# A convolution and feed-forward kernel: the turned filter block in a tile of its own ahead of the weights, taps and D in rows of 64, writes of H and K later

## The chip, the core and the metric

The kernel runs on one core of one Trainium2 chip. The core has five engines with instruction streams of their own: TensorE (PE) multiplies matrices into PSUM, VectorE (DVE) and ScalarE (ACT) do elementwise work and read PSUM, GpSimd (POOL) does small elementwise work and issues transfers, SyncE (SP) only issues transfers. A transfer (DMA) is put into the queue of the engine that issues it, and an engine that waits before an instruction holds everything behind that instruction. The metric is the device time of one execution in microseconds (us); lower is better.

## The reference

```python
def _A_ref(q, k, v, shift_k, ssm_k, ssm_D):       # S = 2048 tokens, D = 576 channels
    k_shift = sum of k moved down by 0..3 tokens, each times its tap shift_k[:, j]
    kv = k_shift * v
    y = causal convolution of kv with ssm_k over the tokens (by a Fourier transform of 2 S)
    return q * (y + kv * ssm_D)

def _B_ref(x, w_gate, w_up, w_down):              # 576 -> 4608 -> 576
    return (_gelu(x @ w_gate) * (x @ w_up)) @ w_down

x = A_q
x = x + _A_ref(_layernorm(x), A_k, A_v, A_shift_k, A_ssm_k, A_ssm_D)
x = x + _B_ref(_layernorm(x), B_w_gate, B_w_up, B_w_down)
x = x + _A_ref(_layernorm(x), A_k, A_v, A_shift_k, A_ssm_k, A_ssm_D)
x = x + _B_ref(_layernorm(x), B_w_gate, B_w_up, B_w_down)
```

(Four lines of it are told in words.) All inputs and the output are bf16. The convolution does not depend on x, so it is computed once and used in both layers.

## The kernel before

The tokens are worked in four blocks of 512 (`BS`), each as four tiles of 128 (`RT`). The convolution is done by blocks: a block of kv and a block of the filter are each taken into a frequency form by matmuls with tables of cosines and sines (`W`, `Wx`), multiplied on VectorE, and brought back by matmuls. The frequency forms are called K (of kv) and H (of the filter); they are kept in DRAM (`Kd`, `Hd`) because later blocks need them again. `kc` and `h0` are the tiles that hold K and H of block 0 until they are written. Block m of the output needs K of the blocks 0 to m and H of the blocks m to 0, and with them two neighbouring products are added.

The feed-forward part goes in units of 512 tokens and one layer, and in three parts (`NP`) of the 4608 hidden columns: twelve tiles of hidden columns are made by matmuls with the gate and up weights (`gu`, L1673 for the first unit's first part, L1755 otherwise), then multiplied by the down weights (`dn`, L1789). The weights are loaded in groups of four tiles, `load_wgu(n)` (three transfers on SP's queue, L1193 to L1195; three buffers) and `load_wd(n)` (L1203).

The program is written by hand in the order in which each engine shall run it. `begin` (L831) is the startup: it makes kv of block 0, H and K of block 0 and the first 512 tokens' gated input, with each matmul and copy in a written order. Then `first_half` (L1601) makes the first half of the first hidden tiles: six steps of 36 matmuls (`half_gu`), for the two tiles of 128 tokens that are ready first; while they run the other two tiles are normalized (`norm0`), turned on TensorE (`turn0`) and copied (`copy0`). The loop of L1739 makes the second half. From there on a planner with estimated costs (`Pace`, `fill`) decides between which matmuls a piece of the convolution of blocks 1 to 3 is put; its decisions are made when the program is built, not while it runs.

The names that the change touches:

- The filter lies in DRAM as channels by tokens. For blocks 1 to 3 it is turned by transposing loads. For block 1 this is done in `begin` (L975 to L981): `hx`, a scratch tile that takes a buffer of `xnT` (the same buffers hold `kT` and `dg` before), takes four transposing loads of 128 tokens in its first half; the result is written to DRAM (`Td[1]`), and read back into its second half in the order of tokens that the matmuls need. `hT1` is that second half. All of these transfers are on SP's queue. `hT1` is first used by the pieces `rest` (L829), the first of which the planner puts behind the first step of the second half; their matmuls are those of L282.
- `head.more(k)` (L1582) issues loads on SP's queue: x of block 0 for k = 0, weight groups 0 and 1 for k = 1, group 2 for k = 2. The down weights are loaded behind `begin` (L1598).
- The taps `shift_k` and the vector D come to one row of `sk1` and `dvec`; twelve matmuls with a one spread the taps of the first 384 channels over the partitions (L889 to L893, copied to `wcol`), two spread those of the last 192 over all partitions (L906, copied to `sx`), five spread D (L914, copied to `dcol`). For the later blocks `taps_out` (L984) reorders the taps on GpSimd by four copies on one row, writes them to DRAM (`skT`), and a transfer spreads them over all partitions (`skc`, L1083). `load_k(1)` and `load_v(1)` load k and v of block 1.
- `put(kt, ...)` (L1021) writes `h0[kt]` or `kc[kt]` to DRAM by a transfer on GpSimd's queue; eight such writes stand in `begin`. `h0[0]` lies in a buffer that the pieces `rest` borrow for their sums, `h0[1]` to `h0[3]` in those of `kr`, into which K is loaded again (L547); `kc` lies in the buffers that K of block 1 takes (L254).

Of the kernel before, what the change touches and what calls it, by code (L numbers as in the profile page):

```python
# [18 lines left out]
BF16 = mybir.dt.bfloat16  # L19
# [3 lines left out]
P = 128  # L23
# [63 lines left out]
class Conv:  # L87
# [743 lines left out]
    def begin(self, head, tables):  # L831
# [4 lines left out]
        with ExitStack() as es:  # L836
            tmp = es.enter_context(tc.tile_pool(name="s_tmp", bufs=1))
            AT = 96
            sk1 = tmp.tile([AT + 1, D, KS], BF16, name="sk1")
            dvec = tmp.tile([1, D], BF16, name="dvec")  # L840
# [5 lines left out]
            ones = tmp.tile([AT + 1, P], BF16, name="ones")  # L846
# [11 lines left out]

            nc.vector.memset(full, 1.0)
            nc.vector.memset(ones[:], 1.0)  # L860
            nc.vector.memset(sk1[0:AT, nt * P:, :], 0.0)
            nc.scalar.dma_start(out=sk1[AT:AT + 1, :, :].rearrange("p d j -> p (d j)"), in_=self.sk.rearrange("d j -> (d j)").unsqueeze(0))
            self.load_k(0, nc.sync)
            nc.scalar.dma_start(out=dvec[:], in_=self.sD.unsqueeze(0))
# [10 lines left out]
            nc.sync.dma_start(out=self.W[:, 12:24, :], in_=tables[:, 12:24, :])  # L875
            head.more(1)

# [11 lines left out]
            for db in range(nt):  # L889
                for j in range(KS):  # L890
                    nc.tensor.matmul(ps[:, 0, db * KS + j:db * KS + j + 1], lhsT=sk1[AT:AT + 1, db * P:(db + 1) * P, j],
                                     rhs=ones[AT:AT + 1, 0:1],
                                     start=True, stop=True)  # L893
            nc.vector.tensor_copy(out=wcol[:].rearrange("p b j -> p (b j)"), in_=ps[:, 0, 0:nt * KS])
# [9 lines left out]
            cuts = ((0, P), (P, DW))  # L904
            for e, (lo, hi) in enumerate(cuts):
                nc.tensor.matmul(ps[:, e, 0:(hi - lo) * KS], lhsT=ones[:], rhs=sk1[:, nt * P + lo:nt * P + hi, :].rearrange("p d j -> p (d j)"),  # L906
                                 start=True, stop=True)
            for e, (lo, hi) in enumerate(cuts):
                nc.scalar.copy(out=sx[:, :, lo:hi], in_=ps[:, e, 0:(hi - lo) * KS].rearrange("p (d j) -> p j d", j=KS))
# [3 lines left out]
            at = DW  # L913
            for db in range(nd + 1):  # L914
                nc.tensor.matmul(px[0:width(db), 1, at + db:at + db + 1], lhsT=dvec[:, db * P:db * P + width(db)], rhs=ones[0:1, 0:1],
                                 start=True, stop=True)
# [12 lines left out]
            nc.scalar.copy(out=kx[:, 2, :], in_=px[:, 1, 0:DW])  # L929
            for dbs, pt in zip(DBS, pts):  # L930
                ne = len(dbs)
                if dbs is DBS[1]:
                    nc.scalar.copy(out=dcol[:, 0:nd], in_=px[:, 1, at:at + nd])
                    nc.scalar.copy(out=dcol[0:D - nd * P, nd:nd + 1], in_=px[0:D - nd * P, 1, at + nd:at + nd + 1])
# [40 lines left out]
            hx = head.scratch([P, 2, RT, D], "hx")  # L975
            for i in range(RT):
                nc.sync.dma_start_transpose(out=hx[:, 0, i:i + 1, :], in_=self.hk[:, BS + i * P:BS + (i + 1) * P])  # L977
            head.more(2)
# [904 lines left out]
```

## Time and profile before

| | us |
|---|---|
| median of 3 runs | 916.75 |
| lowest, highest | 911.25, 917.38 |
| profiled execution, its time | 916.24 |
| profiled execution, span of the core | 914.3 |
| startup up to the first matmul of the feed-forward part | 33.65 |
| wait of TensorE in front of L282 | 4.94 |

The profile is one execution taken by the hardware profiler. Its page gives the busy time of each engine, the queues' transfers and the chain of waits that ended last; further views give the instructions in order of time (the timeline: start, length, engine, line, operation, what it writes and reads, and in brackets the idle time before it and what ended it), who waited for whom, the transfers with their time from issue to landing, and the busy time of each engine in chosen stretches (windows). PE is TensorE's matmuls, PEld its loading of weights; a queue's name ends in q. A line number is that of the kernel before.

### The profile page before, as it was taken

What the parts mean: (1) busy time and instruction counts of PE and PEld (TensorE: products, weight loads), DVE (VectorE), ACT (ScalarE), POOL (GpSimd) and SP (SyncE); (2) the same over time, 40 slices, a digit from 0 to 9 for tenths busy, and PEclk for the clock granted to TensorE, in tenths of its full rate; (3) what the DMA queues carried; (4) which work ended last, traced back from release to release, by engine and by line L of the source; (5) the groups of instructions that cost most, each with busy time, mean ns of one, the idle gap of its engine ahead of it and who ended that gap; (6) DMA issues with size and microseconds to landing.
All of it is one profiled execution on the core that took longest, in us unless ns stands there. A gap on an engine that the chain in (4) does not pass through costs nothing.

```text
span 914.3 us, 19185 instructions
## 1 busy us (share of the span) xinstructions
PE 902.3 (99%) x8143; PEld 525.5 (57%) x8143; DVE 576.8 (63%) x985; ACT 328.9 (36%) x618; POOL 160.2 (18%) x339
## 2 busy tenths in 40 slices
PE   9979999999999999999999999999999999999998
PEld 7766556465565564664655655646646546556555
DVE  8978987679788885697898855443333335333332
ACT  7745534633324255353124133551121224321211
POOL 4502504220114031330114002220000003100000
PEclk9999999999999999999999999999999999999999
DMA  9999995938428508784915700870620721967620
GB/s 250 329 265 236 281 264 116 230 130 195 157 80 226 144 14 150 228 156 99 278 54 127 189 10 32 179 153 20 137 79 2 155 79 27 180 161 175 140 59 27
DMA packets 132025, 132.90 MB, mean 145 GB/s; under 512 B 46114, under 2 KB 123619, under 8 KB 131940
## 3 DMA queue, kind: packets, MB, share of 16 engines
q1 hardware_dynamic: 121728, 94.65, 46.2%
q0 software_dynamic: 10208, 37.02, 12.7%
q8 instruction: 63, 1.03, 0.5%
q14 instruction: 22, 0.18, 0.1%
q10 hardware_dynamic: 4, 0.01, 0.0%
HBM read 108.35 MB, written 12.39 MB: 132 GB/s over the span
## 4 chain that ended last, share of the span: by engine, by line
PE 94%; DMA 4%; DVE 1%; SPq 1%; ACT 0%; issue 0%; ACTq 0%
PE gu L1755 59%; PE dn L1789 31%; DMA Td<-hx 2%; PE gu L1673 1%; DMA hx<-Td 1%; PE cps L282 1%; SPq L977 1%; PE ps L282 1%; DMA hx<-in_A_ssm_k_dram 0%; PE ps L415 0%; PE cps L415 0%; PE cps L885 0%; DVE v L991 0%; DVE wx L948 0%; DVE wx L947 0%; ACT h L1010 0%
## 5 line engine op out<-in xcount | busy, mean ns | idle before, releaser
L1755 PE MATMUL gu<-xnT,wgu 64*128 64x512 bf16 x4968 | 540.7, 377 | 0.0
L1755 PEld LDWEIGHTS <-wgu 64*128 64x128 bf16 x4968 | 240.1, 94 | 293.9 <-issue 6.2
L1764 ACT ACTIVATE ga<-gu 128x512 f32<-128x512 f32 x258 | 153.9, 596 | 451.1 <-PE gu L1755 442.7
L1765 DVE TENSOR_TENSOR hT<-ga,gu 128x512 bf16<-128x512 f32 x258 | 177.1, 687 | 200.4 <-ACT ga L1764 198.9
L1789 PE MATMUL dn<-wd,hT 128*128 128x288 bf16 x2304 | 292.2, 287 | 0.0
L1789 PEld LDWEIGHTS <-hT 128*128 128x128 bf16 x2304 | 223.4, 98 | 65.7 <-issue 9.5
L1828 DVE TENSOR_TENSOR x_c<-x_c,dn 128x576 f32<-128x576 f32 x62 | 46.7, 753 | 55.2 <-PE dn L1789 54.9
L1231 POOL TENSOR_SCALAR nm<-s 128x1 f32<-128x1 f32 x56 | 20.1, 358 | 267.4 <-DVE x_c L1820 210.8
L1239 ACT ACTIVATE junk<-x_c,nm 128x576 bf16<-128x576 f32 x48 | 36.9, 769 | 28.4 <-POOL nm L1231 25.9
L1247 POOL TENSOR_TENSOR rstd<-ve,neghalf_t 128x1 f32<-128x1 f32 x58 | 37.5, 647 | 4.8
L555 POOL DMA_DIRECT2D hr<-Hd x32 | 17.4, 545 | 118.0 <-DVE prod L361 118.0
L1303 ACT ACTIVATE xn<-x_c,nb,rstd 128x576 bf16<-128x576 f32 (+1 forms) x48 | 28.6, 644 | 5.9 <-POOL nb L1251 5.7
L285 ACT COPY eo<-cps 128x576 f32<-128x576 f32 x29 | 18.6, 642 | 31.6 <-PE cps L282 28.3
L1246 POOL TENSOR_SCALAR ve<-ss 128x1 f32<-128x1 f32 x58 | 21.3, 367 | 47.2 <-ACT junk L1239 47.1
L1811 DVE TENSOR_TENSOR ob<-x_c,dn 128x576 bf16<-128x576 f32 x15 | 11.3, 754 | 29.0 <-PE dn L1789 29.0
L1652 ACT ACTIVATE ga<-gu 128x512 bf16<-128x512 f32 x26 | 15.5, 597 | 34.5 <-PE gu L1755 25.9
L1673 PE MATMUL gu<-xnT,wgu 64*128 64x256 bf16 x432 | 26.3, 279 | 0.6 <-ACT xnT L1485 0.6
L1673 PEld LDWEIGHTS <-wgu 64*128 64x128 bf16 x432 | 22.0, 98 | 4.4 <-issue 1.4
L362 DVE TENSOR_TENSOR prod<-prod 128x576 bf16<-128x576 bf16 x48 | 22.0, 458 | 1.7
L430 POOL DMA_DIRECT2D out_dram<-ob x12 | 6.8, 563 | 91.8 <-issue 47.0
L245 DVE SCALAR_TENSOR_TENSOR eo<-eo 128x576 f32<-128x576 f32 x22 | 16.3, 753 | 5.8 <-ACT eo L285 5.8
L1281 DVE SCALAR_TENSOR_TENSOR x_c<-g_t,rstd,x_c 128x576 f32<-128x576 f32 x16 | 13.0, 815 | 8.6 <-POOL rstd L1247 8.6
(188 smaller groups left out, 589.9 us busy)
## 6 DMA issues: line engine op xcount, KB each, us to landing
wgu<-in_B_w_gate_dram SPq DMA_DIRECT2D x45, 576.0 KB, 5.6
wd<-in_B_w_down_dram SPq DMA_DIRECT2D x30, 864.0 KB, 6.8
wgu<-in_B_w_up_dram SPq DMA_DIRECT2D x45, 512.0 KB, 7.9
hr<-Hd POOLq DMA_DIRECT2D x32, 288.0 KB, 4.8
kr<-Kd POOLq DMA_DIRECT2D x24, 288.0 KB, 5.0
Kd<-kc POOLq DMA_DIRECT2D x12, 288.0 KB, 6.3
k<-in_A_k_dram POOLq DMA_DIRECT2D x3, 1008.0 KB, 13.5
wgu<-in_B_w_up_dram SPq DMA_DIRECT2D x45, 64.0 KB, 7.4
```

The source lines that it names most:

```text
L362: nc.vector.tensor_tensor(out=dst, in0=pr[:, 0, :], in1=pr[:, 1, :], op=ALU.subtract if part == 0 else ALU.add)
L1231: nc.gpsimd.tensor_scalar(out=v["nm"][:], in0=v["s"][:], scalar1=-1.0 / D, scalar2=None, op0=ALU.mult)
L1239: nc.scalar.activation(out=junk[:], in_=get_x(), func=ACT.Square, bias=v["nm"][:, 0:1], accum_out=v["ss"][:])
L1246: nc.gpsimd.tensor_scalar(out=ve[:], in0=v["ss"][:], scalar1=1.0 / D, scalar2=EPS, op0=ALU.mult, op1=ALU.add)
L1247: nc.gpsimd.tensor_tensor(out=v["rstd"][:], in0=ve[:], in1=neghalf_t[:, 0:1], op=ALU.pow)
L1303: nc.scalar.activation(out=xn[:, lo:hi], in_=x_c[c][:, j, 0:hi - lo], func=ACT.Identity, scale=v["rstd"][:, 0:1], bias=v["nb"][:, 0:1])
L1673: nc.tensor.matmul(pair[:, s, e * 256:(e + 1) * 256], lhsT=w[r0:r0 + HK, k, gi * P:(gi + 1) * P], rhs=xnT[r0:r0 + HK, blk_of[k], tok], sta ...
L1755: nc.tensor.matmul(pair[:, s, :], lhsT=w[r0:r0 + HK, k, gi * P:(gi + 1) * P], rhs=xnT[r0:r0 + HK, b, :], start=(k == 0), stop=(k == NKC - 1))
L1764: nc.scalar.activation(out=ga[:], in_=pair[:, 0, :], func=ACT.Gelu_apprx_tanh)
L1765: nc.vector.tensor_tensor(out=hT[:, fi, :], in0=ga[:], in1=pair[:, 1, :], op=ALU.mult)
L1789: nc.tensor.matmul(part[h][:, h, 0:HW], lhsT=hT[:, fi, at * P:(at + 1) * P], rhs=wd[2 * wb + fi // WT][:, fi % WT, h * HW:(h + 1) * HW], s ...
L1828: nc.vector.tensor_tensor(out=xh, in0=xh, in1=acc[:, :, 0:HW], op=ALU.add)
```

## The change

The turned filter block gets a tile `hx` of its own, in the startup's pool, so its four transposing loads no longer wait for a buffer. They are issued on SP's queue behind the last table and in front of weight group 0; the write to `Td[1]` follows group 0, and groups 1 and 2 follow the write. The readback stays where it was, in a scratch tile without the first half.

The taps and D are loaded as nine rows of 64 channels, each row twice side by side. Four matmuls with columns of the identity spread the taps of 384 channels (two copies, one for each half of the partitions), three those of the last 192, and D comes by one transpose, with its copies ahead of those of `kT`. `taps_out` is one copy on nine rows, and `load_k(1)` follows it at once. The spread of the taps, `skc`, is issued behind the scales of the first two tiles.

The eight writes of H and K leave `begin`: one is issued in step 1 of `first_half` in the place of `load_x(1)`, four in step 2 behind the accumulating transfers, three in step 2 of the second half, with `load_x(1)` behind them. The two tiles that are turned in steps 2 and 3 of `first_half` are turned in steps 3 and 4.

```diff
-            AT = 96
-            sk1 = tmp.tile([AT + 1, D, KS], BF16, name="sk1")
-            dvec = tmp.tile([1, D], BF16, name="dvec")
+            HP = P // 2
+            NH = D // HP
+            sk9 = tmp.tile([NH, 2, HP * KS], BF16, name="sk9")
+            dv9 = tmp.tile([NH, 2, HP], BF16, name="dv9")
+            sk9t = tmp.tile([NH, KS, HP], BF16, name="sk9t")
+            hx = tmp.tile([P, RT, D], BF16, name="hx")
...
+            nc.scalar.dma_start(out=sk9[:], in_=twice(self.sk.rearrange("(b p) j -> b (p j)", p=HP)))
             self.load_k(0, nc.sync)
-            nc.scalar.dma_start(out=dvec[:], in_=self.sD.unsqueeze(0))
+            nc.scalar.dma_start(out=dv9[:], in_=twice(self.sD.rearrange("(b p) -> b p", p=HP)))
...
             nc.sync.dma_start(out=self.W[:, 12:24, :], in_=tables[:, 12:24, :])
+            for i in range(RT):
+                nc.sync.dma_start_transpose(out=hx[:, i:i + 1, :], in_=self.hk[:, BS + i * P:BS + (i + 1) * P])
             head.more(1)
+            nc.sync.dma_start(out=self.Td[1].rearrange("(t p) d -> p t d", p=P), in_=hx[:])
+            head.more(2)
...
+            for j in range(KS):
+                nc.tensor.matmul(ps[:, 0, 2 * nt * j:2 * nt * (j + 1)], lhsT=sk9[:].rearrange("b h (p j) -> b (h p) j", j=KS)[:, :, j], rhs=self.ident[0:NH, 0:2 * nt], start=True, stop=True)
+            for h, (lo, hi) in enumerate(halves):
+                nc.vector.tensor_copy(out=wcol[lo:hi], in_=ps[lo:hi, 0, 0:2 * nt * KS].rearrange("p (j b h) -> p b j h", b=nt, h=2)[:, :, :, h])
...
+            for c in range(DW // HP):
+                nc.tensor.matmul(ps[:, c // 2, c % 2 * HP * KS:(c % 2 + 1) * HP * KS],
+                                 lhsT=self.ident[0:NH, 2 * nt + c:2 * nt + c + 1].to_broadcast([NH, P]),
+                                 rhs=sk9[:, 0, :], start=True, stop=True)
...
+            nc.tensor.transpose(pt[:, 1, 0:NH], dv9[:].rearrange("b h p -> b (h p)"), self.ident[0:NH, 0:NH])
...
-            hx = head.scratch([P, 2, RT, D], "hx")
-            for i in range(RT):
-                nc.sync.dma_start_transpose(out=hx[:, 0, i:i + 1, :], in_=self.hk[:, BS + i * P:BS + (i + 1) * P])
-            head.more(2)
-            nc.sync.dma_start(out=self.Td[1].rearrange("(t p) d -> p t d", p=P), in_=hx[:, 0])
-            self.hT1 = hx[:, 1]
+            self.hT1 = head.scratch([P, RT, D], "hT1")[:]
             nc.sync.dma_start(out=self.hT1, in_=self.Td[1].rearrange("(p i) d -> p i d", i=RT))
...
-                for j in range(KS):
-                    nc.gpsimd.tensor_copy(out=self.skc[AT:AT + 1, j, :], in_=sk1[AT:AT + 1, :, j])
-                nc.gpsimd.dma_start(out=skT[:], in_=self.skc[AT:AT + 1, :, :].rearrange("p j d -> p (j d)"))
+                nc.gpsimd.tensor_copy(out=sk9t[:], in_=sk9[:, 0, :].rearrange("b (p j) -> b j p", j=KS))
+                nc.gpsimd.dma_start(out=skT[:].rearrange("o (j b p) -> (o b) j p", j=KS, p=HP), in_=sk9t[:])
+                self.load_k(1, nc.gpsimd)
...
             kacc(0)
-            put(0, h0, kc)
-            put(2, h0)
+            nc.gpsimd.dma_start(out=self.skc[:].rearrange("p j d -> p (j d)"), in_=skT[:].broadcast_to([P, KS * D]))
...
+            def put_at(n):
+                for kt, what in (((0, (h0,)),), ((0, (kc,)), (2, (h0, kc)), (1, (h0,))), ((1, (kc,)), (3, (h0, kc))))[n]:
+                    put(kt, *what)
+            self.put_at = put_at
...
-                for n in range(2):
+                load_wgu(0)
+            else:
+                for n in range(1, 3):
                     load_wgu(n)
-            else:
-                load_wgu(2)
...
                     sq0(3)
-                    load_x(1)
+                    conv.put_at(0)
                     root0(3)
-                elif n in (2, 3):
+                elif n in (2, 3, 4):
...
                         conv.together0(conv.A0)
+                        conv.put_at(1)
...
-                    conv.run_p()
-                    j = 2 * n - 3
-                    turn0(j)
-                    copy0(j, nc.scalar.copy)
-                    t.on_act(1.4, t.pe)
+                    if n < 4:
+                        conv.run_p()
+                    if n > 2:
+                        j = 2 * n - 5
+                        turn0(j)
+                        copy0(j, nc.scalar.copy)
+                        t.on_act(1.4, t.pe)
...
                     if n == 0:
                         conv.window = t.pe + 0.6
+                    elif n == 2:
+                        conv.put_at(2)
+                        load_x(1)
```

More of the change, by code (lines that the diff above doesn't have):

```diff
@@ L888, in begin @@
             ps = new()
-            for db in range(nt):
-                for j in range(KS):
[L891 to L894, printed above, removed]
+            halves = ((0, HP), (HP, P))
+            for j in range(KS):
+                nc.tensor.matmul(ps[:, 0, 2 * nt * j:2 * nt * (j + 1)], lhsT=sk9[:].rearrange("b h (p j) -> b (h p) j", j=KS)[:, :, j], rhs=self.ident[0:NH, 0:2 * nt], start=True, stop=True)
+            for h, (lo, hi) in enumerate(halves):
+                nc.vector.tensor_copy(out=wcol[lo:hi], in_=ps[lo:hi, 0, 0:2 * nt * KS].rearrange("p (j b h) -> p b j h", b=nt, h=2)[:, :, :, h])
             def diagonals(db, js=range(KS)):
@@ L903, in begin @@
             ps = new()
[L904 to L908, printed above, removed]
+            for c in range(DW // HP):
+                nc.tensor.matmul(ps[:, c // 2, c % 2 * HP * KS:(c % 2 + 1) * HP * KS],
+                                 lhsT=self.ident[0:NH, 2 * nt + c:2 * nt + c + 1].to_broadcast([NH, P]),
+                                 rhs=sk9[:, 0, :], start=True, stop=True)
+            for e, (lo, hi) in enumerate(((0, P), (P, DW))):
                 nc.scalar.copy(out=sx[:, :, lo:hi], in_=ps[:, e, 0:(hi - lo) * KS].rearrange("p (d j) -> p j d", j=KS))
@@ L912, in begin @@
             px = new()
[L913 to L916, printed above, removed]
             for i in range(KS - 1):
@@ L1075, in begin @@
             kacc(2)
-            put(2, kc)
             kfwd(1, 0, small())
@@ L1082, in begin @@
             kfwd(1, 1, new())
-            nc.gpsimd.dma_start(out=self.skc[:].rearrange("p j d -> p (j d)"), in_=skT[:].broadcast_to([P, KS * D]))
-            self.load_k(1, nc.gpsimd)
             apart(1, 0)
```

15 lines of the change are left out of this document (4 added, 11 removed).

## The prediction

> **What bounds the kernel now.** I read the page first, then who TensorE waits for over the whole span, then the chain of waits around the longest of those waits, then each queue's timeline in the first 90 us. Page, then waits of PE:
>
> ```profile
> span 914.3 us, 19185 instructions
> PE 902.3 (99%) x8143; PEld 525.5 (57%) x8143; DVE 576.8 (63%) x985; ACT 328.9 (36%) x618; POOL 160.2 (18%) x339
> ...
> PE cps L282 <- DMA hx<-Td: 4.9, 1, 4.9
> PE cps L885 <- DVE wx L859: 1.2, 1, 1.2
> PE xps L1478 <- DVE hT L1679: 0.9, 1, 0.9
> PE ps L415 <- DVE yb L362: 0.8, 1, 0.8
> PE gu L1673 <- ACT xnT L1485: 0.6, 1, 0.6
> PE cps L219 <- DVE v L991: 0.3, 1, 0.3
> ```
>
> TensorE is idle for 914.3 − 902.3 = 12.0 us, and the six waits (4.9 + 1.2 + 0.9 + 0.8 + 0.6 + 0.3 = 8.7) are all in the first 56 us; most of the rest is the tail behind the last matmul. So behind the startup only TensorE's own work counts, and this change, which keeps that work, is worth what it does to those waits. The large one, from the chain (start, us, what):
>
> ```profile
> 22.66 4.41 DMA hx<-in_A_ssm_k_dram
> ...
> 27.21 19.40 DMA Td<-hx
> ...
> 46.62 8.34 DMA hx<-Td
> ...
> 55.80 3.54 PE gu L1673 x36
> ...
> 59.69 2.07 PE gu L1673 x36
> ```
>
> The filter block is turned by four transposing loads, written to DRAM (19.40 us for 576 KB), read back (8.34 us) and landed at 46.62 + 8.34 = 54.96. TensorE's next step needed it. Behind the wait the same 36 matmuls took 3.54 instead of 2.07 us. TensorE's timeline gives the wait, and a window the clock (the third number from the end, PEclk):
>
> ```profile
> 55.01 0.40 PE L282 MATMUL cps<-hx,W 128*128 128x288 bf16 x2 [4.94 <-DMA hx<-Td]
> ```
> ```profile
> 55.00:60.00 5.00, 5.00 (x50) 3.21 (x51) 0.00 (x0) 1.79 (x4) 0.00 (x0) 0.66 0.94 338
> ```
>
> TensorE stood from 55.01 − 4.94 = 50.07 on. 5.00 × (1 − 0.66) = 1.70 us of full-speed work is lost to the clock granted after it. The stall costs 4.94 + 1.70 = 6.64 us in all.
>
> **Turned block (L975 to 981).** SP's queue, and three rows of the DMA answer for 27.2 to 46.6:
>
> ```profile
> 4.78 0.65 SPq L1193 DMA_DIRECT2D wgu<-in_B_w_gate_dram  x1
> ...
> 9.07 0.60 SPq L1193 DMA_DIRECT2D wgu<-in_B_w_gate_dram  x1
> ...
> 10.85 3.01 SPq L1195 DMA_DIRECT2D wgu<-in_B_w_up_dram  x1
> 14.04 10.31 SPq L977 DMA_TRANSPOSE hx<-in_A_ssm_k_dram  x4
> ...
> 27.21 1.48 SPq L979 DMA_DIRECT2D Td<-hx  x1
> ```
> ```profile
> q0 software_dynamic: 1286, 4.72, 72.6%
> q1 hardware_dynamic: 1717, 1.76, 30.9%
> ...
> Td<-hx SPq DMA_DIRECT2D x1, 576.0 KB, 19.4
> ```
>
> The write took 19.40 us while POOL's queue (q0) moved 4.72 MB against 1.76 MB of SP's (q1). Before, hx took the buffer of kT and dg and stood in the text behind the work on them. With a tile of its own it follows the last table load, in the place of group 0 of the weights, at 4.78. From first issue to last landing they took 22.66 + 4.41 − 14.04 = 13.03: landed at 17.8. SP issues them until 4.78 + 10.31 = 15.1, then group 0 of the weights (4.78 to 9.07: 4.3 us) until 19.4, so the write of Td goes out at 19.4. Priced as before it lands at 19.4 + 19.40 = 38.8 and the readback at 38.8 + 8.34 = 47.1, still 3 us ahead of 50.07. It should be less, since the eight H and K writes that POOL queued in that stretch are gone from it. I take the wait as gone: **−4.94 and −1.70**. What remains as bound: nothing gone (0) if the write were 3 us longer than 19.40 and everything else as bad.
>
> What the transposes and the write are moved past: groups 0, 1 and 2. Their landing rows of before (groups 1 and 2, last piece), and TensorE's needs:
>
> ```profile
> wgu<-in_B_w_up_dram SPq DMA_DIRECT2D x1, 64.0 KB, 12.5
> wgu<-in_B_w_up_dram SPq DMA_DIRECT2D x1, 64.0 KB, 14.6
> ...
> 33.65 6.15 PE L1673 MATMUL gu<-xnT,wgu 64*128 64x256 bf16 x108 [0.56 <-ACT xnT L1485]
> 40.71 0.66 PE L1478 MATMUL xps<-ident,xn 128*128 128x128 bf16 x9 [0.92 <-DVE hT L1679]
> ```
>
> Two steps of 2.07 use one group. Group 0 is needed at 33.65 and issued by 19.4: 14 us for it. Group 1 is needed at 33.65 + 2 × 2.07 = 37.8; issued behind the write (1.48) from 20.9 on, with its last piece 10.85 − 9.07 = 1.8 later at 22.7, it lands at 22.7 + 12.5 = 35.2. Group 2 goes out 14.04 − 9.07 = 5.0 behind it, last piece at 27.7, lands at 27.7 + 14.6 = 42.3, and is needed at 33.65 + 4 × 2.07 + 0.92 + 0.66 = 43.5. So 1.2 us are to spare at prices of which the 14.6 was paid beside the H and K writes; **0**, bound +2. The down weights, which stood behind SP's wait for Td, come earlier: 0.
>
> A rule bears on this: the Trainium skill, "DMA: Bandwidth & Descriptors", Latency and other measured facts, gives a transposing load 261 GB/s. By it, the block's 576 KB are an estimated 2.3 us, and the weights would slip by that, not 10.3. The trace disagrees (10.31 us of issuing), so the row stands; by the page's figure the weights rival below would all but vanish.
>
> **POOL's queue.** Tap rows, moved steps, the next writer of kc's slots, and landings of H in the crowded stretch and of K over the whole span:
>
> ```profile
> 13.87 2.65 POOL L986 COPY skc<-sk 1x576 bf16<-1x576 bf16 x4
> ...
> 39.12 0.74 POOL L1208 DMA_DIRECT2D x_b<-in_A_q_dram  x1
> ...
> 43.68 2.63 POOL L389 DMA_DIRECT2D yb<-yb  x3 [2.05 <-DVE yb L382]
> 45.30 2.15 POOL L547 DMA_DIRECT2D kr<-Kd  x2
> ...
> 74.16 1.56 DVE L254 TENSOR_TENSOR kc<-eo 128x288 bf16<-128x288 f32 x4
> ```
> ```profile
> Hd<-h POOLq DMA_DIRECT2D x2, 288.0 KB, 14.4
> ...
> Kd<-kc POOLq DMA_DIRECT2D x12, 288.0 KB, 6.3
> ```
>
> Four copies of 0.7 us on one row become one on nine rows (a fifth as many elements per row: bounded by 0.2 and 0.7 us); POOL stands off the chain there, so 0. k of block 1 goes out behind the taps at about 16, the shared taps behind the scales near 23; both are earlier than VectorE needs them, 0. The H and K writes: H of row 0 now goes at 39.12 in the place of x_b. Behind it ACT's first lent tile (slot of h0[0]) is wanted at 50.07 + 0.4; at 14.4 us it would land at 53.5, 3 us late, at an undisturbed few us well ahead. ACT then holds up; TensorE can run on into two further psum pairs (2 × 2.07) before it feels it. 0, bound +1. Four writes follow the accumulating transfers, where the kr loads went (45.30): out at 45.30 + 4 × 0.88 = 48.8 (2.63 / 3 for one issue). Then the first kr load waits on POOL for the K write and for h0[1]'s slot; behind it stand the second kr load, three writes (kc 1, h0[3], kc 3) and x_b of block 1. Landed in 6.3: 55.1, two kr issues (2.15) and three writes (2.6) to 59.9, landed at 66.2; kc's slots are next written at 74.16 − 6.64 = 67.5. So 0, with 1.3 us to spare; at 14.4 for both landings 82.4, 15 late: rival 2. H and K issues also leave 23 to 30, where VectorE's chain runs; 0.
>
> **Startup rows.** Rows of the first matmuls and of what follows:
>
> ```profile
> 3.06 0.56 PE L891 MATMUL ps<-ones,sk 1*128 1x1 bf16 x12
> 4.30 0.40 PE L915 MATMUL ps<-ones,dvec 1*128 1x1 bf16 x5
> ...
> 3.66 0.17 DVE L894 COPY wcol<-ps 128x12 f32<-128x12 f32 x1 [1.79 <-PE ps L891]
> ```
>
> Twelve tap matmuls become four: 8 × (0.49 / 12) = −0.3. One wcol copy becomes two: +0.1 to +0.17. The three matmuls for the taps of the last columns move 768 columns as the two did: 0. The five for D go, one transpose comes, behind the k transposes; the D copies on ACT stand before the kT copies, +0.3 there, hidden by TensorE's h transposes. If nine rows, twice, land later than the one row did: D's row, issued behind the taps, was first used at 4.30, so the taps are there by then against 3.06: +1.2. Ends −0.3 and +1.2; I take **0**, nearest to the matmul rows, which did not wait.
>
> **Turns one step later (L1633).** Step 3's matmuls now take the slot that waited 0.92; that wait stays. Step 3 ends at 40.71 + 2.07 = 42.8, the first turn (0.6) at 43.4, step 4 at 45.45; the second turn then wants the psum slot of step 3, which VectorE frees here:
>
> ```profile
> ...
> 45.13 0.68 DVE L1679 TENSOR_TENSOR hT<-ga,gu 128x512 bf16<-128x512 f32 x1
> ```
>
> 45.13 + 0.68 = 45.81: **+0.36** (0 if VectorE is earlier).
>
> **Sum.** 916.24 (the profiled execution: 914.3 span and 1.94 around it, 0.51 below the median 916.75) − 4.94 − 1.70 + 0.36 = 909.96, so 910.0. What is late next: nothing by 6.64; VectorE, which worked on through the stall, idled 5.72 behind it until TensorE's next products came:
>
> ```profile
> 60.49 0.69 DVE L1656 TENSOR_TENSOR hT<-ga,hT 128x1024 bf16<-128x1024 bf16 x1 [5.72 <-ACT hT L1653]
> ```
>
> That is all but 0.9 of the 6.64, and what it does in the step behind (61 to 68) TensorE wants only one step later.
>
> **Rivals.**
> 1. *Weights late (slower).* SP issues group 1 behind the landing of the transposes, and the transposes stand behind all of the first loads:
>
> ```profile
> W<-twiddles SPq DMA_DIRECT2D x1, 384.0 KB, 8.5
> ```
>
> That last table, issued just ahead of 4.78, landed 8.5 later, at about 12.8. If the transposes move only then and take their 13.03 from there, they land at 25.8, Td goes out at 25.8, group 1 from 27.3 (last piece 29.1), and with 14.6 it lands at 43.7: 5.9 late, and 1.70 of clock: 909.96 + 7.6 = 917.6 (with 12.5, 915.5; with Td's 19.40, 922.4). For: issues of 3.01 us for a piece of 64 KB show that SP's queue backs up. Against: those 13.03 held two groups of weights that were in front, and POOL's eight writes have left the stretch behind. It costs from a landing of group 1 at 37.8 on and turns the sign at 42.4. The Trainium skill, "DMA: Bandwidth & Descriptors", Queues, rings and completion order, says that each DMA engine takes the queues' packets in turn; the row's 72.6 to 30.9 is a worse share for SP than an even turn, so with k, the taps and v in POOL's queue the trace speaks for this rival more than the page does.
> 2. *A new wait behind POOL's queue.* At the lent tile, H of row 0 lands at 53.5: ACT 3 us late, TensorE 1 to 3: 911 to 913. At kc's slots, VectorE is late by what the two landings take beyond 12.6 + 1.3; TensorE goes on for the three psum pairs of down products, 9.3 us (24 matmuls each; the 36 of 2.07 are 18 pairs of half height side by side, so 0.115 for 256 columns and 0.129 for 288); at 14.4 twice 15 − 9.3 and the clock's 1.70, 7.4: 917.4. For: the writes now stand beside the down weights. Against: POOL's queue got the larger share.
> 3. *The wait stays in part.* Td goes out at 25.8 as in rival 1, takes 19.40 and 8.34, and is back at 53.5, or sooner: 1 to 3.4 us late, with some of the clock: 911 to 915. That the change does nothing to the wait: 916.
> 4. *More goes.* VectorE frees the psum slots earlier and the taps' −0.3 come through: −0.36 − 0.92 − 0.3: 908.4, and 907 if the write-free stretch from 23 to 30 gives another us.
>
> **Chances.** Forecast 0.60; rival 1 0.10; rival 2 0.11; rival 3 0.07; rival 4 0.12. The measurement can tell about 1% (9.2 us, 907.6 and 925.9). Faster by over 1%: rival 4 by half, the forecast by a fifth (it needs 2.4 us more): 0.06 + 0.12 = 0.18. Slower by over 1%: rival 1 beyond its 922.4, half of it, 0.05. Within: 0.77. The range goes from 906.5 (rival 4's end with half a us of measurement) to 916 (rival 3 and the first half of 2): rival 1, the second half of 2 and the lower third of 4 are left out, 0.2.
>
> **What would show it.** Right: transposes issued from about 4.8, Td written near 20 and read back before 47; no wait at L282 and PEclk at 1.00 from 50 to 60; wgu issue rows landing before 33.6, 37.8 and 43.5; a short PE wait at L1478 for L1679. Rival 1: PE idle at L1673 by DMA wgu near 37.8. Rival 2: ACT's first L285 waiting for DMA Hd, or VectorE's L254 for DMA Kd. Rival 3: L282 still released by Td's readback. The forecast is wrong if TensorE's waits before 60 us, now 8.7, do not fall to about 4.

## The result, and the profile after

| | before | after |
|---|---|---|
| median, us | 915.83 | 910.36 |
| lowest to highest, us | 910.25 to 917.38 | 910.24 to 916.43 |
| executions | 17 | 17 |
| profiled execution, its time / span, us | 916.24 / 914.3 | 910.27 / 908.5 |

The ratio of after to before is 0.9956, with an interval of 0.994 to 0.9973: a gain of 0.3 to 0.6%. The profiled executions differ by 5.97 us. The two columns differ more in their spread than in their lowest value: 14 of the 17 executions after lie between 910.24 and 910.94, while those of before fill the whole 7 us. One execution named below (928.51, of the scratch kernel) ran in a slower state of the chip; it is in that kernel's range and median, and not in its ratio.

The page of after, and who TensorE waits for over the span (line, total, times, longest); line numbers from here on are those of the kernel in question:

```profile
span 908.5 us, 19158 instructions
PE 900.7 (99%) x8132; PEld 524.3 (58%) x8132; DVE 576.2 (63%) x984; ACT 328.9 (36%) x618; POOL 157.6 (17%) x336
```
```profile
PE cps L890 <- DVE below L867: 1.2, 1, 1.2
PE gu L1670 <- DVE hT L1676: 1.1, 1, 1.1
PE ps L415 <- DVE yb L362: 0.6, 1, 0.6
PE gu L1670 <- ACT xnT L1479: 0.6, 1, 0.6
PE ps L918 <- DMA k<-in_A_k_dram: 0.4, 1, 0.4
PE xps L1472 <- DVE hT L1676: 0.3, 1, 0.3
```

The wait of 4.9 us at L282 is gone; what is left adds up to 4.2 us against 8.7, and the forecast had about 4. The windows of 5 us around the old stall (us, then busy time and count of PE, PEld, DVE, ACT, POOL, then PEclk) and TensorE's timeline show that nothing took its place there and that the clock stayed up: 1.00 where it had been 0.66, and PE busy for all of both windows.

```profile
50.00:55.00 5.00, 5.00 (x82) 3.69 (x78) 4.90 (x8) 3.78 (x7) 0.00 (x0) 1.00 0.78 268
55.00:60.00 5.00, 5.00 (x88) 4.07 (x84) 4.93 (x9) 3.24 (x6) 3.25 (x6) 1.00 1.05 236
```
```profile
33.51 6.15 PE L1670 MATMUL gu<-xnT,wgu 64*128 64x256 bf16 x108 [0.56 <-ACT xnT L1479]
40.74 2.14 PE L1670 MATMUL gu<-xnT,wgu 64*128 64x256 bf16 x36 [1.08 <-DVE hT L1676]
...
45.89 0.66 PE L1472 MATMUL xps<-ident,xn 128*128 128x128 bf16 x9 [0.33 <-DVE hT L1676]
46.49 4.10 PE L1670 MATMUL gu<-xnT,wgu 64*128 64x256 bf16 x72
50.53 0.42 PE L282 MATMUL cps<-hT,W 128*128 128x288 bf16 x2
```

SP's queue after, and one row of the DMA answer (the last number is the time from issue to landing):

```profile
5.10 7.12 SPq L878 DMA_TRANSPOSE hx<-in_A_ssm_k_dram  x4
12.26 0.66 SPq L1187 DMA_DIRECT2D wgu<-in_B_w_gate_dram  x1
...
15.44 0.45 SPq L880 DMA_DIRECT2D Td<-hx  x1
...
24.43 5.22 SPq L1189 DMA_DIRECT2D wgu<-in_B_w_up_dram  x1
29.83 0.46 SPq L977 DMA_DIRECT2D hT<-Td  x1
```
```profile
Td<-hx SPq DMA_DIRECT2D x1, 576.0 KB, 10.1
```

The transposed block is written to DRAM from 15.44 to 15.44 + 10.1 = 25.5. The readback could go then, but SP was still issuing the last piece of weight group 2 until 24.43 + 5.22 = 29.65, so it went at 29.83. The chain of waits has this row for it:

```profile
29.83 10.15 DMA hT<-Td
```

Its end, 29.83 + 10.15 = 39.98, is not the landing. It is the end of a short idle time of VectorE that the chain put down to this transfer. The trace also keeps each update of a semaphore. A transfer makes sixteen, and the last one is its landing: before, the readback's last update is at 54.96, where TensorE's wait ended. After, the sixteen lie between 39.89 and 41.42. So the readback landed at 41.42, against 54.96 before, and 50.53 − 41.42 = 9.1 us ahead of its use. The wait of POOL that the second rival was about is there. POOL's timeline, and the row of VectorE's that could have suffered:

```profile
45.38 1.55 POOL L425 DMA_DIRECT2D Kd<-kc  x1
...
55.20 1.24 POOL L547 DMA_DIRECT2D kr<-Kd  x2 [6.66 <-DMA Hd<-h]
```
```profile
68.08 1.56 DVE L254 TENSOR_TENSOR kc<-eo 128x288 bf16<-128x288 f32 x4
```

POOL waits 6.66 us for the H write before it reloads K. The next writer of kc's slots (DVE, L254) has no wait in its row, so nobody stood behind it.

### The profile page after: what moved, and what is told of

Its sections match the earlier page's. It is cut to its first block, busy times and chain, and to the rows that moved or that the text cites. A ratio compares the mean times of both kernels' runs of the same rounds, so it can differ in the third digit from the quotient of the medians.

```text
span 908.5 us, 19158 instructions
## 1 busy us (share of the span) xinstructions
PE 900.7 (99%) x8132; PEld 524.3 (58%) x8132; DVE 576.2 (63%) x984; ACT 328.9 (36%) x618; POOL 157.6 (17%) x336
## 4 chain that ended last, share of the span: by engine, by line
PE 96%; DVE 2%; DMA 2%; ACT 0%; issue 0%; DVEq 0%; ACTq 0%
PE gu L1755 59%; PE dn L1789 31%; PE gu L1670 2%; DMA hT<-Td 1%; PE cps L282 1%; PE ps L415 1%; PE ps L282 0%; PE cps L415 0%; DVE yb L362 0%; DMA k<-in_A_k_dram 0%; DVE prod L359 0%; DVE h L233 0%; DVE prod L361 0%; PE pt L958 0%; DVE hT L1676 0%; PE cps L818 0%
## 5 line engine op out<-in xcount | busy, mean ns | idle before, releaser
L1789 PE MATMUL dn<-wd,hT 128*128 128x288 bf16 x2304 | 292.1, 286 | 0.0
L1789 PEld LDWEIGHTS <-hT 128*128 128x128 bf16 x2304 | 223.5, 98 | 65.6 <-issue 9.5
L1233 ACT ACTIVATE junk<-x_c,nm 128x576 bf16<-128x576 f32 x48 | 36.9, 768 | 28.3 <-POOL nm L1225 25.8
L555 POOL DMA_DIRECT2D hr<-Hd x32 | 17.5, 546 | 118.6 <-DVE prod L361 118.0
L1240 POOL TENSOR_SCALAR ve<-ss 128x1 f32<-128x1 f32 x58 | 21.6, 373 | 47.3 <-ACT junk L1233 47.1
```

What stands on the lines that cost most here:

```text
L1233: nc.scalar.activation(out=junk[:], in_=get_x(), func=ACT.Square, bias=v["nm"][:, 0:1], accum_out=v["ss"][:])
L1240: nc.gpsimd.tensor_scalar(out=ve[:], in0=v["ss"][:], scalar1=1.0 / D, scalar2=EPS, op0=ALU.mult, op1=ALU.add)
L1789: nc.tensor.matmul(part[h][:, h, 0:HW], lhsT=hT[:, fi, at * P:(at + 1) * P], rhs=wd[2 * wb + fi // WT][:, fi % WT, h * HW:(h + 1) * HW], s ...
```

## The experiments

Ten kernels were run, in three groups, each group on another chip and beside fresh runs of the kernel before. Ratios are to those. Between the groups the median of before moved from 911.78 over 914.04 to 915.87, so medians are compared within a group, and ratios across. The intervals of many ratios overlap; a difference of a few tenths of a percent between two kernels is not shown by them. Where a landing of the readback is given below, it is the last update of its semaphore.

### Which part of the change does it: the place of the block, or the moved writes

The block's early place and the emptied stretch of POOL's queue could each help the write of Td, so each was undone alone, and then both.

*Writes back, block stays ahead:*

```diff
             kacc(0)
+            put(0, h0, kc)
+            put(2, h0)
...
             kacc(2)
+            put(2, kc)
...
             kacc(1)
+            put(1, h0, kc)
+            put(3, h0)
...
+            put(3, kc)
```

> The changed kernel with the eight writes of H and K back in the startup (three from about 23 us, the rest to 30). Theory A (the place of the block ahead of the weights is what removes the stall): Td is written from 15.4 to about 25.5 as in the changed kernel, the readback goes out at 29.8 and lands by 48 even among the writes, before 50.5: 910.3 us, no wait at L282. Theory B (taking the writes out of the stretch is what removes it): the readback takes as long as Td's write did before, 19 us, to 49 and later: a wait again in most runs, 913 to 916 us.

Measured: 910.42 (910.11 to 911.26, 12 executions), ratio 0.9971 (0.9954 to 0.9988). No wait at L282, as with the whole change. SP's queue, and the row of Td's write:

```profile
15.63 0.44 SPq L880 DMA_DIRECT2D Td<-hx  x1
...
34.62 0.47 SPq L977 DMA_DIRECT2D hT<-Td  x1
```
```profile
Td<-hx SPq DMA_DIRECT2D x1, 576.0 KB, 10.0
```

The write of Td takes 10.0 us, as with the whole change. The readback goes out later and lands at 45.29, still 5.3 us ahead of its use at 50.63. So the first theory holds: the writes may stay where they were.

*Block back behind the weights, writes stay late; hx keeps its tile in the startup's pool:*

```diff
-            for i in range(RT):
-                nc.sync.dma_start_transpose(out=hx[:, i:i + 1, :], in_=self.hk[:, BS + i * P:BS + (i + 1) * P])
             head.more(1)
-            nc.sync.dma_start(out=self.Td[1].rearrange("(t p) d -> p t d", p=P), in_=hx[:])
-            head.more(2)
...
             out.append(taps_of(DBS[1], new()))
+            for i in range(RT):
+                nc.sync.dma_start_transpose(out=hx[:, i:i + 1, :], in_=self.hk[:, BS + i * P:BS + (i + 1) * P])
+            head.more(2)
+            nc.sync.dma_start(out=self.Td[1].rearrange("(t p) d -> p t d", p=P), in_=hx[:])
             self.hT1 = head.scratch([P, RT, D], "hT1")[:]
```

(Groups 0 and 1 are loaded together again.)

> The changed kernel with the transposing loads behind weight groups 0 and 1 and Td's write behind group 2, as before the change; hx keeps its own tile and the writes stay late. Theory A: the write of Td goes out at 27 as before, behind group 2, and competes with k, the taps and v only; landing in about 10, readback out at 37 to 40 and back after 10, 47 to 50, so at the limit: 910.3 to 912.5 us. Theory B: without the writes there is no stall at all, 910.3 us with the readback before 45. Theory that only the order on SP's queue counts: 914 to 916 us with the wait of 5 us back.

Measured: 922.11 (921.16 to 922.81, 6 executions), ratio 1.0092 (1.0062 to 1.0123): slower than the kernel before. And both undone:

> Block behind the weights and the writes early: both undone, with the rows of taps and D and the later turns kept. Both theories: the stall is back, 915 to 916.5 us with 4 to 5 us of wait at L282 and the clock at half for 3.4 us. If it stays near 910.3, the gain came from the rows, the early load of k or the turns.

Measured: 932.06 (930.64 to 935.88), ratio 1.0214 (1.0182 to 1.0246). Both results lie far from every number expected. The longest wait of PE in each of the two, and the chain and DVE's timeline of the kernel with the block late, say where:

```profile
PE gu L1670 <- DVE hT L1676: 11.1, 1, 11.1
```
```profile
PE gu L1674 <- DVE hT L1680: 18.6, 1, 18.6
```
```profile
26.26 12.11 DMA hx<-in_A_ssm_k_dram
38.53 11.51 DMA Td<-hx
```
```profile
50.16 2.10 DVE L1676 TENSOR_TENSOR hT<-ga,gu 128x512 bf16<-128x512 f32 x3 [10.24 <-DMA Td<-hx]
```

TensorE no longer waits at L282 but ten us earlier, in step 3 of the first half, for a psum slot. VectorE should have freed it at 40; it stood for 10.24 us until the write of Td had landed (38.53 + 11.51 = 50.04). That instruction writes the first hidden tile hT, which has nothing to do with the filter. The hidden tiles' pool is opened when the startup's is closed, and takes its memory; hx now lies in that memory, so the first hidden product waits for the last reader of hx. So far this is a theory from one row, and there is a second oddity: the transposing loads, issued at 14.88, landed at 26.26 + 12.11 = 38.4, after 23.5 us instead of 13.0.

### Two causes taken apart: hx's memory, and k in the other queue

*The same late block, with hx in the scratch buffer it had before:*

```diff
-            hx = tmp.tile([P, RT, D], BF16, name="hx")
...
+            hx2 = head.scratch([P, 2, RT, D], "hx")
+            hx = hx2[:, 0]
...
-            nc.sync.dma_start(out=self.Td[1].rearrange("(t p) d -> p t d", p=P), in_=hx[:])
-            self.hT1 = head.scratch([P, RT, D], "hT1")[:]
+            nc.sync.dma_start(out=self.Td[1].rearrange("(t p) d -> p t d", p=P), in_=hx)
+            self.hT1 = hx2[:, 1]
```

> Block behind the weights as in e2_block_late, but hx in the scratch buffer that it had before the change instead of the startup's pool. Theory C (the own tile lies under the hidden tiles hT, so VectorE's first product waits for Td's write): the wait of 11 us at step 3 is gone; Td's write still lands near 50, the readback some 7 us later, and TensorE waits at L282 for about 6 us and pays 1.7 of clock: 917 to 919 us. Rival (the late block itself holds step 3 up, wherever it lies): 922 us, with VectorE's first product still waiting for Td.

Measured: 916.81 (912.7 to 928.51, 10 executions), ratio 1.004 (1.0012 to 1.0067). Its waits, and the chain:

```profile
PE cps L282 <- DMA hx<-Td: 3.0, 1, 3.0
...
PE gu L1671 <- DVE hT L1677: 1.0, 1, 1.0
PE gu L1671 <- DMA wgu<-in_B_w_up_dram: 1.0, 1, 1.0
```
```profile
36.98 11.20 DMA Td<-hx
48.19 6.58 DMA hx<-Td
```

The transposing loads are as slow as in the kernel above (issued at 13.73, written out at 36.98), and the write of Td lands at 36.98 + 11.20 = 48.2, long after the 40 us at which VectorE makes its first product. Yet the wait in step 3 falls from 11.1 to 1.0, and the stall is back at L282, with 3.0 us where about 6 were expected. The coupling through the pool's memory is shown: only hx's home (and with it that of the readback) differs.

*The late block in the startup's pool, with k of block 1 and the spread of the taps issued late again:*

```diff
-                self.load_k(1, nc.gpsimd)
...
-            nc.gpsimd.dma_start(out=self.skc[:].rearrange("p j d -> p (j d)"), in_=skT[:].broadcast_to([P, KS * D]))
...
             kfwd(1, 1, new())
+            nc.gpsimd.dma_start(out=self.skc[:].rearrange("p j d -> p (j d)"), in_=skT[:].broadcast_to([P, KS * D]))
+            self.load_k(1, nc.gpsimd)
```

> The kernel with the block behind the weights and in the startup's pool (922.11), with k of block 1 and the spread of the taps back where the kernel before had them, behind the last of the forward transforms, so that about 1 MB less stands in GpSimd's queue between 15 and 26 us. Theory: k and the taps made the transposing loads slow (14.9 to 38.4 us, against 14.0 to 27.1 in the kernel before, where k was issued at 26). Then the loads land by about 28, the write of Td goes out at about 28 and, at 12 to 14 us, lands at about 41, near the 40 us at which VectorE wants its place: a wait of 0 to 3 us at step 3, the readback back by 46 to 50, and 910 to 914. Rival: what is in GpSimd's queue does not matter to the transposing loads, something else in the new order does: they still take over 20 us and the time stays at 920 to 923.

Measured: 914.36 (912.54 to 920.02, 10 executions), ratio 1.0004 (0.9973 to 1.0035), against 922.11 with k early. SP's and POOL's queues, and DVE:

```profile
14.96 9.61 SPq L973 DMA_TRANSPOSE hx<-in_A_ssm_k_dram  x4
...
27.04 0.39 SPq L975 DMA_DIRECT2D Td<-hx  x1
41.61 0.33 SPq L977 DMA_DIRECT2D hT<-Td  x1
```
```profile
26.06 0.54 POOL L176 DMA_DIRECT2D k<-in_A_k_dram  x1
```
```profile
41.66 2.10 DVE L1676 TENSOR_TENSOR hT<-ga,gu 128x512 bf16<-128x512 f32 x3 [1.25 <-DMA Td<-hx]
```

With k's 1008 KB issued at 26.06, the loads were through by 27.04 at the latest, 12.1 us after their issue. In the kernel with k early it went out here, and the spread of the taps only when most of the loads were over:

```profile
15.35 0.60 POOL L176 DMA_DIRECT2D k<-in_A_k_dram  x1
...
32.14 0.63 POOL L1065 DMA_DIRECT2D skc<-skT  x1 [10.63 <-DMA skT<-sk9t]
```

The two kernels differ in k and in the spread. The spread went out at 32.14, when the slow loads had already run for 17 us, longer than all of them took here; so it is k, in the main, that made the transposing loads twice as long. VectorE still waits 1.25 us for Td in this kernel, as its memory demands. The time lies just above the 910 to 914 that were expected.

### Each part alone, in the kernel before

*Only the late writes, in the kernel before:* the eight `put` lines leave `begin`, and `put_at` comes in with its three calls, as in the change.

```diff
-            put(0, h0, kc)
-            put(2, h0)
...
+                        conv.put_at(1)
...
+                    elif n == 2:
+                        conv.put_at(2)
+                        load_x(1)
```

> The kernel before with one part of the change: the eight writes late (and x of block 1 with them); block, rows, k and turns as before. Theory A (the place of the block decides): Td still goes out at 27 and the readback lands near the limit, 910 to 913 us, a wait at L282 left in some runs. Theory B (the writes in POOL's queue are what made Td's write 19 us): it takes about 10, the readback lands by 46 to 47, no wait at L282, 909.8 us (no later turns in this kernel) and little spread.

Measured: 911.31 (910.36 to 916.46, 12 executions), ratio 0.9978 (0.9958 to 0.9999). In the profiled one (910.81) there is no wait at L282:

```profile
27.01 0.53 SPq L979 DMA_DIRECT2D Td<-hx  x1
41.39 0.32 SPq L981 DMA_DIRECT2D hx<-Td  x1
```

The write of Td takes 14.4 instead of 19.4 us, not the 10 of the second theory, and the readback lands at 46.06, 3.9 us ahead of its use. So the late writes alone can remove the stall as well. They do not bring the time down in every execution: four of the twelve lie at 912.79 to 916.46. None of these was profiled, so it is not shown that the same stall is what they have.

*Only the block ahead and the new rows; writes, turns, k, the taps' spread and x where they were:* the edits of the kernel with the writes back and of the one with k late together, with `load_x(1)` and the turns back:

```diff
-                    conv.put_at(0)
+                    load_x(1)
...
-                elif n in (2, 3, 4):
+                elif n in (2, 3):
```

> The other part alone, on the rows of the changed kernel: block in its own tile ahead of the weights, writes early, turns early, k and taps of the later blocks issued where they were before. Theory A: no wait at L282, 909.8 us (910.4 with the later turns, as measured with the writes early, less 0.5). Rival (k's early load matters as well, since it leaves the stretch of the readback): a wait at L282, over 912 us.

Measured: 909.88 (909.51 to 910.34, 12 executions), ratio 0.9966 (0.9951 to 0.9981), in a span of 0.8 us. It is the narrowest of all, and the time is the one that the first theory expected. Its readback goes out 5.5 us earlier than with the whole change:

```profile
14.29 0.44 SPq L880 DMA_DIRECT2D Td<-hx  x1
...
24.31 0.47 SPq L977 DMA_DIRECT2D hT<-Td  x1
```

It lands later all the same, at 44.66 instead of 41.42, in a stretch in which POOL's queue again holds the eight writes, k and the spread; that is 6.0 us ahead of its use at 50.66. The new rows were not run by themselves. They are also in the kernel with the block and k late, which was no faster than the kernel before (1.0004).

*The whole change, with the turns in steps 2 and 3 again:*

```diff
-                elif n in (2, 3, 4):
+                elif n in (2, 3):
...
-                    if n > 2:
-                        j = 2 * n - 5
+                    if n > 1:
+                        j = 2 * n - 3
```

> The changed kernel with the two turns in steps 2 and 3 again. By the step of the prediction that priced the later turns at +0.36 (second turn waits for VectorE's product of step 3; 0.33 in the profile of the changed kernel) 909.9 us, and the wait of 0.33 at the second turn gone, one of about 1.1 left at the first. Rival: the planner's other order costs the same elsewhere, 910.3 us.

Measured: 909.82 (909.75 to 918.66), ratio 0.9981 (0.9958 to 1.0004). Nine of its 12 executions lie below 910.2, seven of them at 909.75 to 909.85, where the kernel with the writes back, in the same group, never came below 910.11 and the whole change never below 910.24: among the quickest executions the later turns cost some 0.4 to 0.5 us. The ratio does not show it, because three executions were slower: 911.00, 911.04 and 918.66. The one at 911.04 is the profiled one; the wait of 0.33 is gone, the one of 1.1 is left, as expected, and there is a new wait for tokens of a later unit:

```profile
PE xps L1472 <- DVE hT L1676: 1.1, 1, 1.1
PE gu L1755 <- DMA xnT<-xn: 0.7, 1, 0.7
```

### The last wait: VectorE's first products

What remains in step 3 is a wait of 1.1 us, because VectorE normalizes two tiles before it makes the product of step 0. In one kernel that product came first, and the planner was told a later time for VectorE:

```diff
                     root0(1)
+                    tail()
                     norm0(1)
-                if n < 4:
+                if 0 < n < 4:
                     tail()
...
-                        t.dve, t.act = t.pe + 2.4, t.pe + 0.6
+                        t.dve, t.act = t.pe + 4.0, t.pe + 0.6
```

> The changed kernel with VectorE's product of step 0 ahead of the normalization of the next tile, and with no kv product put ahead of the product of step 3. If the two waits of TensorE for VectorE in front of the psum slots (1.08 and 0.33 in the profile of the changed kernel) are worth their length: 910.3 - 1.4 = 908.9 us, both waits gone. Rival: the kv products come too late behind them and TensorE waits there, 910.3 us or more.

Measured: 913.13 (908.68 to 917.36, 12 executions), ratio 0.9996 (0.9972 to 1.0019). Three executions came at 908.68 to 908.78 as expected; the other nine lie at 911.39 and above. Both waits are gone from the profiled one (912.83), and a new one stands further on; DVE's and POOL's timelines point to its cause:

```profile
PE dn L1790 <- DVE hT L1654: 2.4, 1, 2.4
```
```profile
91.32 0.76 DVE L359 TENSOR_TENSOR prod<-kc,hr 128x1152 bf16<-128x1152 bf16 x1 [2.31 <-DMA hr<-Hd]
...
96.78 0.76 DVE L359 TENSOR_TENSOR prod<-kc,hr 128x1152 bf16<-128x1152 bf16 x1 [1.47 <-DMA hr<-Hd]
```
```profile
74.62 1.21 POOL L425 DMA_DIRECT2D Hd<-H  x2 [0.85 <-DVE H L249]
80.93 0.55 POOL L555 DMA_DIRECT2D hr<-Hd  x1
```

The order that the planner built with the other estimate reads H back at 80.93; with the estimate of the change it had been 75.41, and 75.54 in the kernel with only the block ahead. VectorE then stands for it twice. To tell the edit from the estimate, the product alone was moved, in the kernel with only the block ahead:

> The kernel with the block ahead alone, and in it the VectorE product of step 0 of the first half goes in front of the normalization of the second tile instead of behind it; the planner's estimates stay as they are, and so the order of the pieces behind. That kernel still has one wait of 1.1 us, where TensorE's step 3 wants a psum slot that VectorE frees late. Theory: VectorE is simply about 1.1 us late with its first products, so the wait goes and nothing takes its place: about 908.8 (909.9 less 1.1), 908.5 to 909.1, and no wait of TensorE over 1.2 us. Rival: whoever reaches the pieces of the convolution 1 us sooner finds H, which GpSimd reads back for block 1 (hr, from Hd), not there yet, as in the run where the estimate was raised too (VectorE stood 2.31 and 1.47 us for it near 90 us, and TensorE then 2.4 us): a wait of 1 to 2.4 us near 100 us and 910 to 912.

Measured: 909.12 (908.92 to 911.33, 10 executions), ratio 0.9945 (0.992 to 0.997). The profiled execution (909.28, span 907.5) reads H back at 74.63 and has no wait over 1.2 us:

```profile
PE cps L890 <- DVE below L867: 1.2, 1, 1.2
PE ps L415 <- DVE yb L362: 0.6, 1, 0.6
PE gu L1675 <- ACT xnT L1483: 0.6, 1, 0.6
```

So the theory holds, with a median 0.02 above the range expected, and the late reading back goes with the estimate. As the two kernels also differ in where the eight writes stand, this is not the estimate taken entirely by itself. The median was the lowest of all kernels. The time against the whole change was not measured in one group; its lowest is 908.92 against 910.24.

## Why the prediction came out right, and where it did not see

**The stall, −4.94.** Gone, as the forecast had it. The reason given, that the block starts ahead of the weights, is shown by the kernel with the block alone: no stall, and twelve executions within 0.8 us. The second reason, that the eight writes leave the stretch, was not needed: with them back in place the write of Td took 10.0 us and nothing waited. It is not without effect either: alone, in the kernel before, the late writes took the stall out of the profiled execution. The late block in the scratch buffer has a stall of 3.0, but k runs beside its loads there, so it does not tell the place of the block from k. The single prices were off in both directions. The loads took 7.12 us to issue, not 10.31, Td went out at 15.44, not 19.4, and landed in 10.1, not 19.40. The readback lost 4.3 us behind SP's own issue of the weights, which the working did not have, and took 41.42 − 29.83 = 11.6 us instead of 8.34. It was back at 41.42, not 47.1. A transfer that is in time costs nothing, so these errors left no mark on the sum. That is in part luck: from the working's 38.8 for Td, the readback's 11.6 would have ended at 50.4, just behind the 50.07 at which TensorE wanted it. The 9.1 us to spare come from loads and a write that were much cheaper than priced.

**The clock, −1.70.** From L282 to the first `dn` matmul (L1789) it took 68.75 − 55.01 = 13.74 us before and 62.67 − 50.53 = 12.14 after: −1.60.

**The later turns, +0.36.** The second turn waits 0.33. The kernel with the turns back finds 0.4 to 0.5 in its lowest times: a cost, and whether the later turns buy anything is open, since that kernel also has the wait of 0.7 and the execution at 918.66.

**Startup rows, 0.** The first `gu` matmul starts at 33.51 instead of 33.65: −0.14. It brought nothing, because the slot that is next wanted came no earlier: VectorE's products started at 40.00 instead of 39.98, with 0.19 us of idle time in front, and the wait in step 3 grew from 0.92 to 1.08. The trace names the readback as what ended those 0.19 us, but they are 0.19 in the kernel with the writes back too, where the readback was issued 4.8 us later and a weight load is named. They go with the number of semaphores that the instruction waits for: 0.03 us with five (before), 0.09 with six (the scratch kernel), 0.19 with eight (after, and in the kernels with the writes back, with the block alone and with the turns back). So they are probably a small price of hx's new home; no run tests that alone.

**Weights and POOL, 0.** No wait for `wgu` or behind POOL's writes. Group 1's last piece landed at 17.26 + 17.5 = 34.8 and was wanted at 33.51 + 2 × 2.07 = 37.65; group 2's landed at 24.43 + 15.8 = 40.2 and was wanted at 43.42. Rivals 1 and 3 both had the transposing loads land at 25.8; they had landed by 15.44. In weighing rival 1, the prediction set the queues' shares of time (72.6 to 30.9) against an even turn by packets. Counted in packets, the same row gives SP's queue 1717 to POOL's 1286, so it does not show that SP's queue got fewer turns. K's reload was foreseen at 55.1 and came at 55.20; the next write to kc's slots at 67.5 and came at 68.08. The weights rival is seen in small only where k runs beside the late block (1.0 us for `wgu` in the scratch kernel).

**The fourth rival, more goes.** Not in this change: the psum slots came free no earlier. The last kernel shows that it was there to have, as VectorE's product moved in front takes the wait of 1.08 away and 0.8 us off the median of the kernel with the block alone, as far as medians of two groups can be set side by side.

**The sum.** −4.94 − 1.60 + 0.33 − 0.14 + 0.16 = −6.19 for what has a name; TensorE's last group of down matmuls starts 899.10 − 893.02 = 6.08 us earlier, and the profiled times differ by 5.97, against 6.28 forecast. The gain over many executions is smaller, a ratio of 0.9956 or some 4 us, because the stall is not in every execution of before: there are executions at 910.25, with no room for a stall of 6.6. The granted clock fits: of the executions of before that ran beside the experiments, nearly all above 914 us have 0.996 to 0.998 over the whole span, as the profiled one has (0.998), and all below 913 have 0.999 or 1.000. The working took the stall for a constant; it is a transfer that lands near the time of its use, sometimes before. The trace of before was one execution and could not show that, but the three times beside it (911.25 to 917.38) could have.

**What no rival had.** The tile of hx's own has a price: the first hidden product waits for its last reader. It is next to nothing here, as Td is written by 25.5 and the product starts at 40.00. Late, it was worth 11 us. And the early load of k, taken at 0, is free only because the transposing loads are through when it goes out at 15.28. So these parts hang together: the block ahead is what makes the tile's home and the early k harmless.

**Open.** Single long executions remain after (916.43 once in 17, 912.13 once) and with the turns back (918.66). None of them was profiled. The two longest have a granted clock of 0.996, so TensorE's clock was lowered in them too, as behind a long wait; where they wait is not known. That the spread of before comes from the readback is not shown by a trace of a long and a short execution. Nor do the landings of the profiled executions order the kernels: the readback lands at 40.98 with the turns back (8.9 us between lowest and highest), 41.42 with the whole change (6.2), 44.66 with the block alone (0.8), 45.29 with the writes back (1.2), 46.06 with the late writes alone (6.1), 54.96 before (7.1). The two that land first have the outliers, so something else can lengthen an execution as well.

## What to carry to other kernels

A spread of a few us between executions can be a transfer that lands close to its use: look for the wait, and start that chain of transfers earlier, before clearing the way for it. The end of a short wait that a profile puts down to a transfer need not be that transfer's landing. When a tile gets a home in another pool, ask which later tile takes that memory, and who then waits for the last reader. Where a planner's estimates set the order of the work, move an instruction without touching them first; the order that a new estimate builds may read something back too late.

## What the runs showed of the hardware

The same four transposing loads (576 KB) took 7.12 us to issue and 9.15 to land (5.10 to 14.25, the last update of the fourth load's semaphore) when they followed the first loads and ran ahead of the weights, about 12 us beside weights and small transfers, and 23.5 us when a load of 1008 KB in POOL's queue was issued just behind them. The Trainium skill, "DMA: Bandwidth & Descriptors", Latency and other measured facts, gives 261 GB/s for a transposing load; here 589,824 bytes in 9.15 us are 64 GB/s and in 23.5 us 25 GB/s, so no run here came near it. In that last kernel the 4.5 KB of the taps, issued in POOL's queue at 14.55, took 17.3 us to land; in the whole change they took 6.6 us.
